# Six passes of a left output projection move forward by one place each, and their sum is copied in the fifth phase of a segment in place of the sixth

## The chip, the cores and the metric

The kernel runs on one core of a Trainium2 chip. The metric is the device time of one execution in microseconds (us), of which the median of several runs is taken. Engines are named as the profile names them: PE is the matrix engine (PEld its weight loads), DVE the vector engine, ACT the scalar engine, POOL the general engine that here mostly issues small transfers, SP the engine that issues the stream of weights.

## The reference, cut to what matters

The output is the sum of a normalised input, a recurrent attention over segments (branch A) and a small routed feed-forward layer for two rows (branch B, which ends the program and is not touched).

```python
xn = layernorm(x)                                  # x: 2048 rows of 1024, bf16
mem = mem0                                         # 8 rows of 1024
for s in range(64):                                # 64 segments of 32 rows
    h = concat([mem, xn[32*s:32*s+32]])            # 40 rows
    q, k, v = h @ Wq, h @ Wk, h @ Wv               # 32 heads of 128, each W is 1024 x 4096
    p = softmax(mask(q k^T * scale))
    o = (p v) @ Wo                                 # Wo is 4096 x 1024
    mem = o[:8]                                    # goes into the next segment
    outs.append(o[8:])
out = x + concat(outs) + B(xn)                     # A and B both take xn
```

A segment needs the memory that the segment before it has produced, so the 64 segments run one after another. The rows that no later segment needs can be computed at another time.

## The kernel before

**Main and left rows.** Of the 40 rows of a segment, 32 go through the main path in their own segment: the 8 memory rows and the first 24 of the 32 new rows. The last 8 new rows of each segment, the *left* rows, are gathered over four segments into a group of 32 rows and taken through the same weights as extra passes, spread over the segments. `G, j = divmod(s, 4)` gives the group G and the place j of a segment s in it.

**Weights.** The four matrices are cut into 64 granules of 128 x 2048 (512 KB each): granules 0 to 47 are the six halves of Wq, Wk and Wv, 48 to 63 are Wo. 44 of them stay in the chip's memory for the whole program (tiles `wres`). The other 20 are streamed: SP fetches them again in every segment, in the fixed order of `STREAMED`, into a ring of `N_SLOT = 5` slots (tile `g`, line 354; one granule, 6, and half of 25 are kept elsewhere and copied back). A slot is refilled as soon as the last pass that reads it has run on PE. The wait for a free slot stands in SP's queue.

**A segment on PE.** Phases 0 to 5 run over 8 granules each (line 788, into `PSm`, four matmuls a granule); then comes the stage of the output projection over granules 48 to 63 (`project`, line 574, into `WO`), in which the second half of the attention is done (`attend`, w = 5 and 8). A place in the program is written (phase, granule of the phase). After w = 15, DVE adds the sum to the input (line 856), PE turns the result (line 293), DVE writes the memory rows into `ST` (line 316), and the next segment's phase 0 can begin.

**Extra passes.** `PASSES` puts the left rows' passes at places `(j, phase, granule)`. A pass of q, k or v is four matmuls (`left_pass`, line 567, into `PSl`, with `STL` as the stationary operand); a pass of the output projection is eight matmuls of 256 columns (line 574, into `WL`, with `OTL`). The unit "o" has sixteen such passes: ten in segment j = 3 and the last six (granules 55, 57, 58, 60, 61 and 63, all resident) in the next segment, j = 0. PSl and WL are the same single buffer in turn. Phases 7 and 8 in the table stand for two places between the segments: the three passes (0, 7, 0) of "q0" run after w = 15, before PE turns the result, and the two at (0, 8, 0) after it.

**The copy of "o".** `COPIES` names the place where a finished unit is copied. For "o" (`copy_unit`, lines 594 to 599) DVE adds `WL` to the tile `OL`, which holds the input rows, and POOL then issues four DMAs (line 599) that write `OL` to the output. `OL` lies in the place (tag `"stl"`) that the next group's `STL` takes: ACT writes `STL` (line 311) in the output stage of segment j = 0 at w = 8, and may only do so when the four DMAs of line 599 have landed. Behind line 311 stand, on ACT, two copies that bring granule 6 back (line 377), and on PE the passes (0, 7, 0), which read `STL`. This meeting of the old `OL` and the new `STL` occurs at 14 group boundaries (s = 4, 8, ..., 56).

**What sets the order.** Each engine runs its instructions in the order in which this code issues them. `hook(phase, granule, fn)` puts work behind a granule. On DVE and ACT those of interest in j = 0 are: `scores(0)` at (2, 6), `exponent` and `soften(0)` at (3, 4), `scores(1)` at (4, 6), `exponent` and `soften(1)` at (5, 0), `attend(0, ..)` at (5, 4) and (5, 6). `soften` ends on DVE with line 694, `scores` begins there with line 656.

Of the kernel before, what the change touches and what calls it, by code (L numbers as in the profile page):

```python
# [43 lines left out]
}  # L44

COPIES = {"q0": (1, 1, 0, "scalar"), "q1": (1, 5, 7, "vector"), "k0": (2, 2, 0, "scalar"), "k1": (3, 1, 0, "scalar"),
          "v0": (3, 4, 7, "scalar"), "v1": (3, 5, 7, "scalar"), "o": (0, 5, 3, "vector")}


@with_exitstack  # L50
# [933 lines left out]
```

## Time and profile before

| | us |
|---|---|
| median of three runs | 1922.05 |
| the three runs | 1922.05, 1910.76, 1924.17 |
| profiled execution, its own time | 1913.83 |
| its span, from the first to the last instruction | 1912.2 |
| PE busy in the span | 1577.0 (82%) |
| DVE busy | 879.8 (46%) |
| ACT busy | 682.0 (36%) |
| POOL busy | 442.1 (23%) |

All 16 DMA engines together moved 712.41 MB, 373 GB/s in the mean; 671.18 MB of that went through SP's queue. The profile gives the clock that PE was granted (PEclk) and the DMA engines' busy share for any stretch of time. In the timeline a row is: start, duration, engine, line, operation, tile written and tiles read, and in brackets how long the engine stood idle before it and what ended that. A row of the waits view is: who waited, for whom, total us, times, longest.

### The profile page before, as it was taken

To read this page: it belongs to the slowest core of one execution; us is meant where nothing else is said; L and a number is where in the kernel's file an instruction comes from. 1 tells how busy PE (TensorE), PEld (TensorE's weight loads), DVE (VectorE), ACT (ScalarE), POOL (GpSimd) and SP (SyncE) were. 2 spreads that over 40 slices of the span, in tenths; PEclk is the share of its full clock that TensorE was granted. 3 is DMA by queue.
4 is the path that set the end of the run, shared out by engine and by line. 5 is a ranking of instruction groups with operands and counts; after the bars stand their busy time and mean duration, and the time that the engine had idled before them with its cause. 6 is when DMAs were issued, how large, how long until landed. Compare 5 with 4: busy or idle time off the path is not lost.

```text
span 1912.2 us, 82457 instructions
## 1 busy us (share of the span) xinstructions
PE 1577.0 (82%) x36000; PEld 877.3 (46%) x36000; DVE 879.8 (46%) x2913; ACT 682.0 (36%) x1916; POOL 442.1 (23%) x882
## 2 busy tenths in 40 slices
PE   3468889898888888888898888889898888889864
PEld 1134545454444544445454544545454544545433
DVE  6734544444444444444553454355444444445430
ACT  1123343343333333333343333334343433334320
POOL 3111312222131222213122211312132121312220
PEclk8669999999999999999999999999999999999995
DMA  9999999999999999999999999999999999999998
GB/s 371 402 363 387 371 378 377 361 377 349 386 364 362 366 385 377 345 383 369 380 382 342 388 362 373 340 386 371 379 384 381 373 373 379 368 376 384 388 388 334
DMA packets 232122, 712.41 MB, mean 373 GB/s; under 512 B 39296, under 2 KB 53168, under 8 KB 231760
## 3 DMA queue, kind: packets, MB, share of 16 engines
q1 hardware_dynamic: 194384, 671.18, 92.3%
q0 software_dynamic: 28736, 28.09, 4.6%
q10 hardware_dynamic: 8640, 7.87, 1.2%
q8 instruction: 282, 4.62, 0.9%
q14 instruction: 80, 0.66, 0.1%
HBM read 694.32 MB, written 22.29 MB: 375 GB/s over the span
## 4 chain that ended last, share of the span: by engine, by line
DMA 55%; PE 39%; DVE 3%; issue 2%; ACT 0%; SPq 0%; ACTq 0%; DVEq 0%
DMA g<-wsc 44%; PE PSm L788 20%; PE PSl L567 6%; PE WO L574 5%; DMA out_dram<-OL 4%; PE BT L624 3%; PE WL L574 2%; DMA XP<-in_A_x_dram 2%; DMA MW<-in_B_w_gate_dram 1%; DVE XR L248 1%; DMA MW<-in_B_w_up_dram 1%; DMA g<-in_A_Wq_dram 1%; DMA wres<-in_A_Wo_dram 1%; PE BT L293 1%; DMA g<-in_A_Wo_dram 1%
## 5 line engine op out<-in xcount | busy, mean ns | idle before, releaser
L788 PE MATMUL PSm<-wres,ST 128*32 128x512 bf16 x8448 | 700.0, 385 | 6.1 <-issue 2.3
L788 PEld LDWEIGHTS <-ST 128*32 128x32 bf16 x12288 | 325.8, 96 | 411.3 <-issue 177.9
L788 PE MATMUL PSm<-g,ST 128*32 128x512 bf16 x3588 | 362.0, 387 | 109.8 <-DMA g<-wsc 85.2
L574 PEld LDWEIGHTS <-OT 128*32 128x32 bf16 x8192 | 218.3, 97 | 153.2 <-issue 134.4
L807 ACT CAST XB<-PSm 128x512 bf16<-128x512 f32 x256 | 150.5, 588 | 320.2 <-PE PSm L788 318.4
L574 PE MATMUL WO<-wres,OT 128*32 128x256 bf16 x5632 | 239.7, 278 | 24.3 <-issue 14.2
L483 POOL DMA_DIRECT2D LX<-ql_d x63 | 33.7, 535 | 766.4 <-PE WO L574 398.1
L567 PE MATMUL PSl<-wres,STL 128*32 128x512 bf16 x2112 | 189.4, 401 | 25.5 <-ACT STL L311 25.2
L574 PE MATMUL WO<-g,OT 128*32 128x256 bf16 x2560 | 133.6, 281 | 71.0 <-DMA g<-wsc 57.2
L858 POOL DMA_DIRECT2D out_dram<-X x256 | 129.7, 514 | 209.5 <-DVE X L856 169.5
L273 POOL DMA_DIRECT2D X<-in_A_x_dram x256 | 129.6, 511 | 187.5 <-PE PSm L788 77.6
L639 DVE COPY KT<-BT 128x512 bf16<-128x512 bf16 x112 | 45.7, 408 | 265.0 <-ACT XB L807 115.9
L567 PEld LDWEIGHTS <-STL 128*32 128x32 bf16 x3072 | 82.7, 99 | 88.5 <-ACT STL L311 29.1
L632 ACT COPY QT<-BT 128x512 bf16<-128x512 bf16 x128 | 75.0, 586 | 113.9 <-PE BT L490 62.0
L377 ACT COPY BK<-KEPT 128x512 bf16<-128x512 bf16 x126 | 72.8, 591 | 107.6 <-PE WO L574 94.4
L624 PEld LDWEIGHTS <-XB 128*128 128x128 bf16 x1024 | 58.5, 98 | 108.1 <-ACT XB L807 68.8
L817 ACT CAST VM<-PSm 128x512 bf16<-128x512 f32 x128 | 75.8, 592 | 89.4 <-PE PSm L788 87.6
L856 DVE TENSOR_TENSOR X<-WO,X 128x256 bf16<-128x256 f32 x64 | 27.2, 425 | 171.8 <-PE WO L574 171.8
L710 PEld LDWEIGHTS <-VM 32*128 32x128 bf16 x2048 | 65.1, 91 | 84.9 <-issue 70.1
L624 PE MATMUL BT<-IDENT,XB 128*128 128x128 bf16 x1024 | 102.1, 222 | 1.9 <-ACT QKL L502 1.4
L381 DVE COPY g<-KEPT 128x512 bf16<-128x512 bf16 x126 | 47.6, 419 | 119.4 <-PE PSm L788 76.0
L656 DVE TENSOR_TENSOR BS<-BS,CT 128x96 f32<-128x96 f32 (+1 forms) x256 | 59.5, 233 | 91.6 <-PE BS L649 87.2
(171 smaller groups left out, 2360.7 us busy)
## 6 DMA issues: line engine op xcount, KB each, us to landing
g<-wsc SPq DMA_DIRECT2D x1134, 512.0 KB, 6.1
g<-wsc SPq DMA_DIRECT2D x63, 256.0 KB, 5.1
LX<-ql_d POOLq DMA_DIRECT2D x63, 128.0 KB, 5.9
ql_d<-XBl ACTq DMA_DIRECT2D x60, 128.0 KB, 5.8
MW<-in_B_w_gate_dram SPq DMA_DIRECT2D x16, 448.0 KB, 9.1
MW<-in_B_w_up_dram SPq DMA_DIRECT2D x16, 448.0 KB, 9.3
wres<-in_A_Wk_dram SPq DMA_DIRECT2D x12, 512.0 KB, 11.3
MW<-in_B_w_down_dram SPq DMA_DIRECT2D x12, 512.0 KB, 10.2
```

The lines of the kernel that those rows point to most:

```text
L273: nc.gpsimd.dma_start(out=X[s % 2][32 * g:32 * g + XM, :], in_=x2[s * SEG:s * SEG + XM, 256 * g:256 * (g + 1)])
L377: copy(out=back[c][:, :], in_=KEPT_COLS[KEPT_WHOLE][c])
L567: nc.tensor.matmul(PSl[32 * jq:32 * jq + 32, :], lhsT=STL[:, g % KC, :], rhs=part(Gv, jq), start=first_, stop=last_, tile_position=(0, 32 ...
L574: nc.tensor.matmul(PS[32 * g:32 * g + 32, 0:256], lhsT=lhs(h), rhs=Gv[:, D * hs + 256 * g:D * hs + 256 * (g + 1)], start=(first and hs == ...
L624: nc.tensor.transpose(out=PTq[:, il, :, :].rearrange("p j r -> p (j r)"), in_=XB[:, il * P:(il + 1) * P], identity=IDENT[:, :])
L632: nc.scalar.copy(out=QT[half][:, :, :], in_=pv)
L656: nc.vector.tensor_tensor(out=S4, in0=S4, in1=m, op=ALU.add)
L710: nc.tensor.matmul(o, lhsT=VM[half][q0:q0 + 32, il * P:(il + 1) * P], rhs=PTm[q0:q0 + 32, il, 0:NK], start=True, stop=False, tile_position ...
L788: nc.tensor.matmul(PSm[32 * jq:32 * jq + 32, :], lhsT=ST[:, kc, :], rhs=part(Gv, jq), start=(kc == 0), stop=(kc == KC - 1), tile_position= ...
L807: nc.scalar.copy(out=XB[:, :], in_=PSm[:, :])
L817: nc.scalar.copy(out=VM[half][:, :], in_=PSm[:, :])
L858: nc.gpsimd.dma_start(out=out2[s * SEG:s * SEG + XM, 256 * g:256 * (g + 1)], in_=OB[32 * g:32 * g + XM, :])
```

## The change

It edits two tables. In "o", six places of j = 0 are exchanged: granule 55 runs behind (1, 5) where it ran behind (2, 4), 57 behind (2, 2) for (3, 0), 58 behind (2, 5) for (3, 4), 60 behind (3, 2) for (4, 2), 61 behind (3, 5) for (4, 6), and 63 behind (4, 2) for (5, 1). The copy of "o" moves from (5, 3) to (4, 3).

```diff
-          (3, 8, 0): [52, 54], (0, 2, 4): [55], (0, 3, 0): [57], (0, 3, 4): [58], (0, 4, 2): [60], (0, 4, 6): [61],
-          (0, 5, 1): [63]},
+          (3, 8, 0): [52, 54], (0, 1, 5): [55], (0, 2, 2): [57], (0, 2, 5): [58], (0, 3, 2): [60], (0, 3, 5): [61],
+          (0, 4, 2): [63]},
...
-          "v0": (3, 4, 7, "scalar"), "v1": (3, 5, 7, "scalar"), "o": (0, 5, 3, "vector")}
+          "v0": (3, 4, 7, "scalar"), "v1": (3, 5, 7, "scalar"), "o": (0, 4, 3, "vector")}
```

No instruction is added or taken away. The rows on POOL, ACT and SP keep their order; those on PE and DVE move. On DVE, segment s = 4 before the change, from the end of `soften(0)` on (BS holds the scores, PT and BX the probabilities, OL the rows of the output, WL the sum of the sixteen passes):

```order
L656 TENSOR_TENSOR BS<-BS,CT 128x4x24
L658 TENSOR_SCALAR BS<-BS,CT 128x4x8
L656 TENSOR_TENSOR BS<-BS,CT 128x4x8
L661 TENSOR_REDUCE NM<-BS 128x8
L662 TENSOR_TENSOR BS<-BS,NM 128x320
L671 TENSOR_REDUCE DN<-BS 128x8
L672 RECIPROCAL DN<-DN 128x8
L678 TENSOR_TENSOR PT_3978<-BS,DN 128x256
L690 TENSOR_TENSOR BX<-BS,DN 128x8x8
L692 STREAM_TRANSPOSE PT_3978<-PT_3978 128x256
L694 STREAM_TRANSPOSE PT_3978<-BX 128x256
L596 TENSOR_TENSOR OL<-WL,OL 128x256
```

The addition of line 596 stands behind all of `scores(1)` and `soften(1)`. The same place of the changed kernel:

```order
L692 STREAM_TRANSPOSE PT_3854<-PT_3854 128x256
L694 STREAM_TRANSPOSE PT_3854<-BX 128x256
L596 TENSOR_TENSOR OL<-WL,OL 128x256
L656 TENSOR_TENSOR BS<-BS,CT 128x4x24
L658 TENSOR_SCALAR BS<-BS,CT 128x4x8
```

It now stands directly behind `soften(0)` and ahead of `scores(1)`: eleven instructions have gone from in front of it to behind it. On PE, segment s = 4 before, the last of the sixteen passes stands behind granule 41 (of its eight pairs of rows one is shown, as of the granules):

```order
L788 LDWEIGHTS ST_3438
L788 MATMUL PSm_3969<-wres41_827,ST_3438 32x512
L574 LDWEIGHTS OTL_650
L574 MATMUL WL_3342<-wres63_1237,OTL_650 32x256
L788 MATMUL PSm_3969<-g_3855,ST_3438 32x512
```

The same pass in the changed kernel:

```order
L788 LDWEIGHTS ST_3438
L788 MATMUL PSm_3883<-wres34_663,ST_3438 32x512
L574 LDWEIGHTS OTL_650
L574 MATMUL WL_3342<-wres63_1237,OTL_650 32x256
L788 MATMUL PSm_3883<-wres35_681,ST_3438 32x512
```

It has gone ahead of seven granules of the main path. At any place between (1, 5) and (5, 1) the changed kernel has run one or two more passes of "o" than the kernel before.

## The prediction

> **What bounds the kernel now.** I read the page first: the engines' shares and the chain that ended last.
>
> ```profile
> PEclk8669999999999999999999999999999999999995
> DMA  9999999999999999999999999999999999999998
> DMA 55%; PE 39%; DVE 3%; issue 2%; ACT 0%; SPq 0%; ACTq 0%; DVEq 0%
> ```
>
> The DMA engines are busy nearly all the time and more than half of the chain is the weight stream. PE waits for it in many short pieces. So time can be won only where the stream itself stands still, that is where PE has not freed a slot. The waits view names candidates:
>
> ```profile
> PE PSm L788 <- DMA g<-wsc: 85.2, 179, 1.7
> ACT STL L311 <- DMA out_dram<-OL: 50.1, 14, 5.0
> PE PSl L567 <- ACT STL L311: 25.2, 14, 3.2
> PEld L293 <- DVE X L856: 18.9, 44, 1.0
> PEld L788 <- DVE ST L316: 15.9, 49, 0.6
> ```
>
> Rows two and three are one event at the 14 group boundaries: ACT may not write the new STL before the four output DMAs of the old OL have landed (3.6 us in the mean), and PE then stands 25.2 / 14 = 1.8 us before the passes at (0, 7, 0). The timelines of DVE, POOL, ACT and PE show the boundary of segment 8:
>
> ```profile
> 333.44 0.45 DVE L694 STREAM_TRANSPOSE PT<-BX 128x256 bf16<-128x256 bf16 x1
> 334.74 0.27 DVE L656 TENSOR_TENSOR BS<-BS,CT 128x96 f32<-128x96 f32 x1 [0.85 <-PE BS L649]
> 338.79 0.45 DVE L694 STREAM_TRANSPOSE PT<-BX 128x256 bf16<-128x256 bf16 x1
> 339.15 0.38 DVE L596 TENSOR_TENSOR OL<-WL,OL 128x256 bf16<-128x256 f32 x1
> ...
> 339.83 2.40 POOL L599 DMA_DIRECT2D out_dram<-OL  x4 [9.47 <-DVE RI L268]
> ...
> 343.08 0.32 ACT L307 COPY ST<-BT 128x192 bf16<-128x192 bf16 x1 [0.46 <-DVE OTL L721]
> 348.07 0.37 ACT L311 COPY STL<-BT 128x256 bf16<-128x256 bf16 x1 [4.67 <-DMA out_dram<-OL]
> ...
> 348.50 1.47 PE L567 MATMUL PSl<-wres,STL 128*32 128x512 bf16 x12 [2.98 <-ACT STL L311]
> ```
>
> The addition (L596) runs the moment `soften(1)` is done on DVE; POOL issues 0.7 us later; the last issue ends at 342.23 and the last landing is 5.8 us behind it; ACT had been ready at 343.40. Now whether the stream stands still there: the busy time by stretches, 12 us from each of the 14 writes of STL on. The columns are span, length, busy us of PE, PEld, DVE, ACT, POOL, then PE's granted clock, the DMA engines' share, GB/s.
>
> ```profile
> 238.80:250.80 12.00, 11.25 (x218) 5.38 (x222) 3.42 (x10) 5.45 (x12) 4.38 (x9) 1.00 1.00 354
> 348.10:360.10 12.00, 11.60 (x201) 5.13 (x202) 2.69 (x9) 4.85 (x10) 2.56 (x6) 0.86 0.73 265
> 458.10:470.10 12.00, 11.57 (x181) 4.83 (x184) 1.70 (x5) 4.28 (x9) 3.17 (x7) 0.74 0.69 243
> 570.20:582.20 12.00, 11.59 (x202) 5.16 (x202) 2.80 (x9) 4.85 (x10) 3.08 (x7) 0.86 0.79 250
> 679.90:691.90 12.00, 11.61 (x226) 5.61 (x230) 3.59 (x11) 5.92 (x13) 4.39 (x9) 1.00 0.99 351
> 788.80:800.80 12.00, 11.62 (x162) 4.72 (x166) 1.70 (x5) 4.26 (x9) 3.60 (x8) 0.73 0.74 243
> 900.10:912.10 12.00, 11.58 (x222) 5.50 (x223) 3.56 (x11) 5.92 (x13) 4.39 (x9) 1.00 0.96 327
> 1009.40:1021.40 12.00, 11.61 (x199) 5.10 (x200) 2.56 (x9) 4.83 (x10) 2.30 (x5) 0.86 0.71 242
> 1119.30:1131.30 12.00, 11.61 (x199) 5.04 (x200) 2.59 (x9) 4.83 (x10) 3.77 (x8) 0.86 0.83 284
> 1231.80:1243.80 12.00, 11.53 (x198) 5.01 (x198) 2.48 (x9) 4.88 (x10) 4.39 (x9) 0.86 0.93 312
> 1342.00:1354.00 12.00, 11.53 (x226) 5.68 (x230) 3.51 (x11) 5.88 (x13) 4.38 (x9) 1.00 0.98 339
> 1449.00:1461.00 12.00, 11.40 (x222) 5.50 (x223) 3.42 (x10) 5.71 (x12) 3.88 (x9) 1.00 0.93 321
> 1557.60:1569.60 12.00, 11.57 (x222) 5.50 (x223) 3.54 (x11) 5.92 (x13) 4.38 (x9) 1.00 1.01 366
> 1666.80:1678.80 12.00, 11.55 (x226) 5.67 (x230) 3.53 (x11) 5.90 (x13) 3.11 (x7) 1.00 0.94 313
> ```
>
> Two things stand in these rows. The stream does stand still, and in seven of them PE's clock is below 1: its clock was halved for about (1 - 0.86) x 2 x 12 = 3.4 us (twice as long in two rows), right behind PE's stand. What a saturated share reads in this trace is seen 14 to 6 us ahead of the same boundaries, of which one row and the sum are:
>
> ```profile
> 556.20:564.20 8.00, 7.25 (x217) 4.67 (x208) 6.02 (x23) 3.34 (x14) 2.37 (x4) 1.00 1.02 406
> sum 112.00, PE 91.92 PEld 56.68 DVE 84.00 ACT 49.84 POOL 20.00; mean PE 6.57 PEld 4.05 DVE 6.00 ACT 3.56 POOL 1.43
> ```
>
> Against 1.02 the 14 rows lose 14 x 1.02 - 12.23 = 2.05, times 12 us = **24.6 us** of streaming: 20.6 us in the seven with a halved clock (2.9 each), 4.0 us in the others (0.57 each). That is all this place can give.
>
> **The change, part by part.**
>
> *The addition and its four DMAs.* The new place of L596 is behind the first `soften` and ahead of `scores(1)`. In segment 8 it can start where the first L694 lets it, 338.79 - 333.44 = 5.35 us earlier. WL must be complete by then, 333.80: the pass behind (4, 2) ran at 332.38, and a pass takes PE 0.22 us (its row and PE's next one):
>
> ```profile
> 332.38 0.39 PE L574 MATMUL WL<-wres,OTL 128*32 128x256 bf16 x8
> 332.60 0.39 PE L788 MATMUL PSm<-wres,ST 128*32 128x512 bf16 x4
> ```
>
> With two more passes ahead of that point, WL is done at 332.38 + 0.39 + 2 x 0.22 = 333.2. Queued behind L596 on DVE are the masks of `scores(1)` (L656), for which DVE waits 0.85 us anyway; 0.38 us fit in. POOL has nothing between load_seg at (2, 4) and L599 and waited there for 9.47 us, so the issues move by the full 5.35 us and end at 336.9. With the same 5.8 us the last landing is at 342.7, 0.7 us ahead of ACT at 343.4. The longest of the 14 waits was 5.0 us, so the same shift, taken for all, covers every one; I know the soften ends of this boundary alone. If the wait stayed in part, each us of it would cost what it costs now.
>
> *What is late next.* Without the stall PE goes straight through the passes (7, 0). Behind them it needs X from L856 and then ST from L316. The two PEld rows above price these waits at the other boundaries: 18.9 / 44 = 0.43 us and 15.9 / 49 = 0.32 us. They are now partly hidden under the stall and will show up here. So PE does not win the whole 1.8 us, and I do not take the loss of streaming to zero: what is left is between 0.12 us (the row with share 1.01) and the 0.57 us of the seven unhalved rows; I take 0.35 us, in the middle. 14 x 0.35 = 4.9 us remain, **19.7 us** go.
>
> *The clock.* This sum takes the halving to go with the stand. The rows speak for it: all seven lowered clocks lie right behind the stand of PE. They do not follow from its length alone, since 0.97 us was followed by one and 2.48 us by none (the row of 1666.80 has clock 1.00):
>
> ```profile
> 1232.27 1.04 PE L567 MATMUL PSl<-wres,STL 128*32 128x512 bf16 x8 [0.97 <-ACT STL L311]
> 1667.24 0.83 PE L567 MATMUL PSl<-wres,STL 128*32 128x512 bf16 x12 [2.48 <-ACT STL L311]
> ```
>
> PE's other short waits for the stream count too, and those stay. I leave one boundary in 14 halved: 2.9 - 0.57 = **+2.4 us** (bounds: none; three, 7.1).
>
> The Trainium skill has a rule on this that speaks against the change: the page "TensorE: Matmul & The Clock Gate", section "HAM oscillation — how this bites in real kernels", says "The abstract rule is "no PE-idle gaps >~3.4µs."" By that rule gaps of 0.9 to 3.2 us halve nothing, and only the unhalved part of the loss would go, about 3 us. The trace does not agree: the clock fell behind stands of 2.98 and 0.97 us.
>
> *The moved passes.* Between (1, 5) and (5, 1) PE has run one or two passes more than before, so each slot there is freed up to 2 x 0.22 = 0.44 us later, in 15 segments. At (5, 1) all is as before. Where the stream has reserves this costs nothing. In the stretch 24 to 16 us ahead of the boundary, where the first passes now fall, PE has little idle time, and in two of 14 boundaries the stream was already short:
>
> ```profile
> 1207.80:1215.80 8.00, 8.00 (x173) 4.79 (x168) 3.43 (x13) 3.48 (x7) 4.66 (x9) 0.96 0.82 258
> 1318.00:1326.00 8.00, 8.00 (x180) 4.33 (x176) 3.65 (x13) 3.46 (x7) 4.65 (x9) 1.00 0.82 277
> sum 112.00, PE 108.67 PEld 58.81 DVE 48.00 ACT 50.00 POOL 63.55; mean PE 7.76 PEld 4.20 DVE 3.43 ACT 3.57 POOL 4.54
> ```
>
> The bounds are 0 (the stream is saturated, so PE's earlier work can gain nothing there either) and 15 x 0.44 = 6.6 us. I take the two short ones, 2 x 0.44, **+0.9 us**. `scores(0)` and `soften(0)` come up to 0.44 us later with them, which is within the 0.7 us above.
>
> **The sum** against the profiled execution's 1913.83 us: -19.7 + 2.4 + 0.9 = -16.4, so **1897.4 us**. The median of the three runs, 1922.05, is 8.2 us above that execution. Their spread of 13.4 us is what five or six halved boundaries more or less would make at 2.4 us each (an estimate), and that is the term that goes; so I add nothing for it to the middle, only to the top of the range.
>
> **The rivals.**
>
> *The halving stays.* If what halves the clock is PE's many short waits for the stream, which sum to 6.57 busy of 8 us ahead of the boundary, the seven stay halved and only 14 x (0.57 - 0.35) = 3.1 us go: 1910.7. For it: the 0.97 us row. Against it: the other 50 boundaries between segments have the same waits, and the page's clock line (PEclk, tenths) stays at 9 from the first segments on. Chance 0.11.
>
> *The stall stays or another takes its place.* The margin is 0.7 us in segment 8; a landing that takes 1 us longer beside another piece of the stream would keep part of it. Or PE is held by L856 and L316 for as long as by STL. Then nothing is gained and the passes cost up to 6.6 us: 1911 to 1920, 1914 if both are small. Chance 0.13.
>
> *Slower: the clock halves at every boundary.* Three passes (those of 60, 61, 63) leave the stretch 14 to 6 us ahead of the boundary, where PE idles (112 - 91.92) / 14 = 1.43 us of 8; it would idle 1.43 + 0.66 = 2.1 us. If that is what tips the clock, all 14 are halved in place of seven: 7 x 2.4 = 16.8 us more, 1930.6 against the profiled time, 1938.9 on the scale of the median. It decides from the point at which the stretch before the boundary shows clocks under 1 in most segments, which now it does not. Chance 0.04.
>
> That the change does not do what it says is excluded by the order of the rows on DVE and PE.
>
> **How the numbers follow.** Forecast 0.70, the rivals 0.11, 0.13 and 0.04, anything else 0.02. The forecast's own range is 1887 (all 24.6 us and 2 us of other waits) to 1908 (three halved, 4.7 us more, and 6.6 us for the passes, 5.7 more). Eight in ten are held by 1887 to 1912, which takes in the first rival and the lower edge of the second. A measurement of this kernel can tell about 1% from no change; 1% below 1922.05 is 1902.8, which about 0.60 of the forecast's 0.70 stay under. The other 0.10 and the first two rivals lie within 1%, as does most of the third. Faster 0.62, within 1% 0.34, slower 0.04.
>
> **What would show it.** Right: no row of ACT L311 waiting for out_dram<-OL; L596 ahead of the second L656 and some 5 us earlier; PE's wait for STL gone from the waits view and L293 waiting for X at up to 58 places in place of 44; in the 12 us behind the writes of STL shares of 0.96 and more and clocks of 1.00. Wrong: shares as now with clocks of 1.00 (another bound), halved clocks without a stall (the first rival), shares well under 1 in the stretch 24 to 16 us ahead (the passes cost more), or L311 still waiting.

## The result, and the profile after

The changed kernel takes 1895.51 us (median of five runs, 1883.18 to 1900.43), the kernel before 1924.10 us (1910.76 to 1924.51): a ratio of 0.9856 with a 95% interval of 0.9807 to 0.9905, 28.6 us less. The profiled execution took 1889.55 us with a span of 1887.9 us, 24.3 us less than the one of before. A ratio here is taken over the undisturbed runs alone, so it need not be the quotient of the medians; in the first round of experiments (before: 1923.38 us) the seven slowest of the nineteen runs of the kernel before are left out as disturbed, so the ratios of that round lean high.

From the page and the waits view of the changed kernel, the lines that answer to those of before:

```profile
PEclk8669999999999999999999999999999999999995
DMA  9999999999999999999999999999999999999998
DMA 57%; PE 38%; DVE 2%; issue 2%; SPq 0%; ACT 0%; ACTq 0%; DVEq 0%
...
POOL out_dram L599 <- DVE OL L596: 90.1, 15, 8.0
PE PSm L788 <- DMA g<-wsc: 75.5, 172, 2.6
PEld L293 <- DVE X L856: 24.5, 58, 1.0
PEld L788 <- DVE ST L316: 16.1, 49, 0.6
```

No row is left in which ACT or PE waits for OL or STL. The wait of PE's weight loads for X has gone from 44 places to 58: the 14 boundaries now show what the stall had hidden. The timelines of DVE, POOL, ACT and PE at the boundary of segment 8:

```profile
333.66 0.45 DVE L694 STREAM_TRANSPOSE PT<-BX 128x256 bf16<-128x256 bf16 x1
334.03 0.39 DVE L596 TENSOR_TENSOR OL<-WL,OL 128x256 bf16<-128x256 f32 x1
334.95 0.27 DVE L656 TENSOR_TENSOR BS<-BS,CT 128x96 f32<-128x96 f32 x1 [0.54 <-PE BS L649]
339.00 0.45 DVE L694 STREAM_TRANSPOSE PT<-BX 128x256 bf16<-128x256 bf16 x1
...
334.70 2.40 POOL L599 DMA_DIRECT2D out_dram<-OL  x4 [4.29 <-DVE OL L596]
...
343.84 0.32 ACT L307 COPY ST<-BT 128x192 bf16<-128x192 bf16 x1 [0.46 <-DVE OTL L721]
344.05 0.38 ACT L311 COPY STL<-BT 128x256 bf16<-128x256 bf16 x1
...
346.00 0.83 PE L567 MATMUL PSl<-wres,STL 128*32 128x512 bf16 x12
```

The addition runs as the first `soften` ends, 339.00 - 333.66 = 5.34 us ahead of the end of the second, and still leaves DVE 0.54 us of waiting before the masks. ACT writes STL right behind ST. PE goes from the output projection into the passes without a stand, and its twelve matmuls take 0.83 us where they took 1.47. The stretches of 12 us from each write of STL on (columns as before):

```profile
237.00:249.00 12.00, 10.76 (x206) 5.67 (x209) 2.15 (x7) 4.45 (x10) 4.52 (x10) 1.00 1.00 371
344.10:356.10 12.00, 11.38 (x238) 5.97 (x237) 2.83 (x9) 4.93 (x11) 4.43 (x10) 1.00 1.02 383
449.90:461.90 12.00, 10.55 (x226) 5.58 (x229) 2.15 (x7) 4.34 (x9) 4.38 (x9) 1.00 1.02 387
559.90:571.90 12.00, 10.75 (x234) 5.83 (x233) 2.43 (x8) 4.49 (x11) 4.47 (x10) 1.00 1.01 383
668.20:680.20 12.00, 11.47 (x238) 5.92 (x237) 2.90 (x10) 4.92 (x11) 4.42 (x10) 1.00 1.03 387
775.60:787.60 12.00, 11.28 (x238) 5.84 (x237) 2.65 (x9) 4.73 (x11) 4.49 (x10) 1.00 1.03 390
882.30:894.30 12.00, 10.38 (x226) 5.50 (x224) 2.18 (x7) 4.41 (x10) 4.49 (x10) 1.00 1.03 391
989.00:1001.00 12.00, 10.21 (x186) 4.99 (x185) 2.16 (x7) 4.40 (x10) 3.58 (x8) 1.00 1.02 385
1100.10:1112.10 12.00, 12.00 (x242) 6.38 (x234) 2.19 (x8) 4.41 (x10) 4.38 (x9) 0.86 0.92 310
1210.90:1222.90 12.00, 10.70 (x230) 5.71 (x229) 2.31 (x8) 4.40 (x10) 4.49 (x10) 1.00 1.03 399
1319.00:1331.00 12.00, 12.00 (x241) 6.64 (x234) 2.44 (x8) 4.52 (x11) 4.42 (x10) 0.88 0.93 315
1427.90:1439.90 12.00, 11.84 (x238) 6.28 (x234) 2.21 (x7) 4.44 (x10) 4.37 (x9) 0.87 0.93 309
1535.70:1547.70 12.00, 11.12 (x238) 6.02 (x237) 2.67 (x9) 4.76 (x11) 4.46 (x10) 1.00 1.02 386
1642.80:1654.80 12.00, 11.53 (x247) 6.14 (x246) 2.92 (x10) 5.01 (x11) 4.50 (x10) 1.00 1.03 401
```

The shares sum to 14.02 where they summed to 12.23, and three stretches show a lowered clock where seven did. Against a full share of 1.02 that is a loss of (14.28 - 14.02) x 12 = 3.1 us in place of 24.6. The last column says more: its mean goes from 300.7 to 371.2 GB/s, which over 14 x 12 us is 11.8 MB, and at the changed kernel's mean of 377 GB/s 31.4 us of streaming. The two readings of the same stretches differ by 10 us, because the busy share does not count how fast a busy engine moves: 300.7 GB/s at a mean share of 0.87 before, 371.2 at 1.00 after. The spans of the two profiled executions differ by 24.3 us, which lies between the two. The DMA view of the kernel before and then of the changed one, over 12 us from the start of the next segment's phase 0 at 351.1 and at 347.4 us (the first digits are the busy share in 40 slices, the second row GB/s):

```profile
DMA  1200001783999788974899999999999899989988
GB/s 72 85 27 27 0 0 41 89 130 123 437 369 423 291 331 331 239 130 150 335 434 365 403 362 386 362 389 382 382 355 382 341 396 396 437 341 369 369 314 328
```

```profile
DMA  9999999999999999999999999998999999989999
GB/s 423 369 287 341 369 382 396 410 423 396 430 355 379 403 413 386 399 341 376 410 396 437 389 389 413 420 393 355 382 413 423 379 430 396 382 352 423 382 396 410
```

Before, the stream all but stands for seven slices of 0.3 us, and in the two behind them the engines are 0.7 and 0.8 busy at only 89 and 130 GB/s.

### The profile page after: what moved, and what is told of

Its sections match the earlier page's. It is cut to its first block, busy times and chain, and to the rows that moved or that the text cites. A ratio compares the mean times of both kernels' runs of the same rounds, so it can differ in the third digit from the quotient of the medians.

```text
span 1887.9 us, 82457 instructions
## 1 busy us (share of the span) xinstructions
PE 1574.1 (83%) x36000; PEld 882.6 (47%) x36000; DVE 880.0 (47%) x2913; ACT 681.9 (36%) x1916; POOL 441.4 (23%) x882
## 4 chain that ended last, share of the span: by engine, by line
DMA 57%; PE 38%; DVE 2%; issue 2%; SPq 0%; ACT 0%; ACTq 0%; DVEq 0%
DMA g<-wsc 50%; PE PSm L788 21%; PE PSl L567 5%; PE WO L574 5%; PE BT L624 3%; PE WL L574 2%; DMA XP<-in_A_x_dram 2%; DMA MW<-in_B_w_gate_dram 1%; DMA MW<-in_B_w_up_dram 1%; DVE XR L248 1%; DMA g<-in_A_Wq_dram 1%; DMA wres<-in_A_Wo_dram 1%; DMA g<-in_B_w_down_dram 1%; DMA g<-in_A_Wo_dram 1%; PE BT L293 1%
## 5 line engine op out<-in xcount | busy, mean ns | idle before, releaser
L567 PE MATMUL PSl<-wres,STL 128*32 128x512 bf16 x2112 | 184.2, 389 | 0.0
```

What stands on the lines that cost most here:

```text
L567: nc.tensor.matmul(PSl[32 * jq:32 * jq + 32, :], lhsT=STL[:, g % KC, :], rhs=part(Gv, jq), start=first_, stop=last_, tile_position=(0, 32 ...
```

## The experiments

The theory: four output DMAs that land late hold back the write of STL, PE stands behind it and frees no slots, and the stream starves. The rivals: the gain comes from where the six passes lie; the halved clock, not the stand, is what costs; or the clock falls for another reason. Beside most runs stands the mean GB/s over its 14 stretches of 12 us from the start of phase 0 of j = 1 (before 306, changed kernel 371), a figure worked out from 14 rows like the one quoted.

**The wait alone.** The kernel before, with nothing moved, but OL in a place of its own (lines are left out at the marks; one of them keeps granule 0's room from being used again in the last segment):

```diff
+SHORT = 0
...
+        if g == SHORT:
+            t = home(g, [P, 1536], BF16, f"wres{g}")
+            nc.sync.dma_start(out=t[:, :], in_=granule_dram(g)[:, 0:1536])
...
+        if t is res_tiles.get(SHORT):
+            jq = min(jq, 2)
...
-                xl_of[0] = load_left(G, one.tile([P, 256], BF16, tag="stl", name="OL")[:, :])
+                xl_of[0] = load_left(G, one.tile([P, 256], BF16, tag="ol", name="OL")[:, :])
```

> The kernel before, with no pass and no copy moved; OL alone gets a place of its own, so that the write of STL has no output DMA to wait for. Room for it is made by keeping only 1536 of the 2048 columns of granule 0, whose last quarter of matmuls reads the third quarter's columns instead (that part of the product is left out). Theory (the wait of STL for the landing of OL's DMAs is the whole cost): ACT's wait at line 311 for OL and PE's 25 us of waiting for STL are gone, the 12 us behind the writes of STL show DMA shares of 0.96 and more, and the time is 16 to 20 us under the kernel before, ratio 0.985 to 0.991, as with the change. Rival (the gain comes from where the passes lie): ratio 0.998 to 1.002.

Measured: 1881.93 us against 1923.38, ratio 0.9805 (0.9748 to 0.9862), and 372 GB/s. At segment 8:

```profile
347.80:359.80 12.00, 11.11 (x220) 5.62 (x220) 3.81 (x12) 5.02 (x10) 3.87 (x9) 1.00 1.02 375
```

So the wait is the whole of the gain; moving the passes and the copy is one way to be rid of it, and not needed for it. The ratio is under the range that I had given: the wait is worth more than the 16 to 20 us that I had taken, 26 us at the least by the interval.

**The passes alone.** The changed kernel's passes, with the copy at its old place:

```diff
-          "v0": (3, 4, 7, "scalar"), "v1": (3, 5, 7, "scalar"), "o": (0, 4, 3, "vector")}
+          "v0": (3, 4, 7, "scalar"), "v1": (3, 5, 7, "scalar"), "o": (0, 5, 3, "vector")}
```

> The six passes at their new places, the copy of o left behind (5, 3). Theory: DVE still adds behind the second soften, the DMAs land as late as before, the stall and about seven halved boundaries stay; the passes cost 0 to 6.6 us: ratio 1.000 to 1.004. Rival (the passes are what gains): ratio 0.985 to 0.99.

Measured: 1928.50 us against 1923.38, ratio 1.0040 (1.0009 to 1.0070), 296 GB/s. Its waits view:

```profile
ACT STL L311 <- DMA out_dram<-OL: 47.9, 14, 4.7
PE PSl L567 <- ACT STL L311: 27.3, 14, 3.5
```

The stall is all there. The rival falls: the passes gain nothing. By the ratio they cost 0.1 to 0.7% beside the late copy, but this is one of the ratios that lean high; the medians of all runs differ by 5 us, and the trace shows nine of the 14 boundaries with a lowered clock where the kernel before shows seven. So that they cost anything is not shown.

**Fewer passes.** Copy behind (4, 3), passes 55, 57 and 58 at their old places (the diff is against the changed kernel):

```diff
-          (3, 8, 0): [52, 54], (0, 1, 5): [55], (0, 2, 2): [57], (0, 2, 5): [58], (0, 3, 2): [60], (0, 3, 5): [61],
+          (3, 8, 0): [52, 54], (0, 2, 4): [55], (0, 3, 0): [57], (0, 3, 4): [58], (0, 3, 7): [60], (0, 4, 1): [61],
```

> The copy behind (4, 3) as in the change, but passes 55, 57 and 58 stay at their old places; 60 goes to (3, 7), 61 to (4, 1) and 63 to (4, 2), the least that lets the sum be whole at (4, 3). Theory: the gain hangs on the copy, so it is all there, and what the early passes cost (0.9 us taken, 6.6 at most) comes on top: ratio 0.983 to 0.987, at most 6 us under the change. Rival (the early passes fill PE where it would idle): slower than the change by 3 us or more, ratio 0.988 and up.

Measured: 1888.85 us, ratio 0.9823 (0.9771 to 0.9875). All of the gain is there, a little more than expected; whether more than the change gives, the interval does not say.

**PE filled while it stands.** The kernel before, with work for PE that is thrown away:

```diff
+        if j == 0 and s > 0 and G + 1 < NT:
+            begin("q0")
+            for i in range(N_FILL):
+                for jq in range(4):
+                    nc.tensor.matmul(units["q0"][0][32 * jq:32 * jq + 32, :], lhsT=lhs_main(31),
+                                     rhs=part(res_tiles[0], jq), start=True, stop=True, tile_position=(0, 32 * jq))
         run_passes(7, 0)
```

> The kernel before with 20 matmuls of 512 columns put in front of the passes (7, 0) at the 14 boundaries; they write the bank that the first of these passes overwrites, so no sum changes. At full clock they fill 1.1 us of PE's stand of 1.8 us (mean). The write of STL comes as late as before. Theory (PE's stand lowers the clock): the remaining stand is 0.7 us in the mean, halved boundaries fall from seven to three or fewer, time 8 to 12 us under the kernel before, ratio 0.994 to 0.996. Rival (the clock is lowered by PE's short waits for the stream, not by this stand): six or more halved boundaries, ratio 0.999 to 1.003.

Measured: 1912.88 us against 1923.38, ratio 0.9986 (0.9951 to 1.0021), 321 GB/s. The waits view (lines are one further down in this kernel) and the stretch behind segment 8:

```profile
ACT STL L312 <- DMA out_dram<-OL: 50.5, 14, 4.8
PE PSl L568 <- ACT STL L312: 10.0, 11, 2.0
...
348.50:360.50 12.00, 11.11 (x223) 5.51 (x220) 5.03 (x15) 5.02 (x10) 2.00 (x4) 1.00 0.97 334
```

ACT waits as long as before, PE stands for 10.0 us in place of 25.2, and of the 14 stretches one shows a lowered clock, where in the same stretches of the kernel before seven do. So it is PE's standing that lowers the clock at these boundaries, and the rival that it falls for another reason goes. All ten runs bear it out: their mean clock is 0.956, that of the 19 runs of the kernel before 0.949. The time is inconclusive: the interval of the ratio holds part of what the theory and part of what the rival expected, while the medians of all runs differ by 10.5 us (0.9945), as the theory had it.

**The change again, and smaller ones beside it.** On one chip: the changed kernel, the kernels of "Fewer passes" and "The wait alone" once more, and the kernel before with pass 63 one place earlier and the copy in the gap between `scores(1)` and `soften(1)`:

```diff
-          (0, 5, 1): [63]},
+          (0, 4, 7): [63]},
...
-          "v0": (3, 4, 7, "scalar"), "v1": (3, 5, 7, "scalar"), "o": (0, 5, 3, "vector")}
+          "v0": (3, 4, 7, "scalar"), "v1": (3, 5, 7, "scalar"), "o": (0, 5, 0, "vector")}
```

> The changed kernel once more, as the measure for the three below on the same chip. Theory (the early passes cost streaming in phases 0 to 4 of j = 0): ratio 0.984 to 0.988, the slowest of the four. Rival (passes cost nothing, the four differ by chance): all four ratios within 0.003 of each other.

> Only passes 60, 61 and 63 moved, copy behind (4, 3), as in two_moved. Theory: passes 55, 57 and 58 stay where they were, so the part of the cost that lies in phases 1 and 2 goes: 3 to 6 us under after_again, ratio 0.981 to 0.984. Rival (no cost): within 0.003 of after_again.

> OL in a place of its own and every pass and the copy where they were in the kernel before, as in own_place (the last quarter of granule 0's product is taken with the third quarter's columns). Theory: no stall and no moved pass, so the fastest of the four, 7 to 13 us under after_again, ratio 0.979 to 0.982. Rival (no cost): within 0.003 of after_again.

> The kernel before with only two edits: pass 63 goes from (5, 1) to (4, 7), one place, and the copy of o from (5, 3) to (5, 0), where its addition stands on DVE between scores(1) and soften(1), in a gap of 0.49 us that DVE has there. The addition comes 339.15 - 336.60 = 2.5 us earlier in the trace of before, half of what the change gives. ACT's waits of 1.6 to 5.0 us at line 311 shrink to 0 to 2.5 us (15 us in all), PE's stand of up to 3.2 us to 0.7 us at most. Theory (only PE's stand costs): all but 1 us of the stand is gone and hardly a pass is moved, ratio 0.980 to 0.984, at or under two_again. Rival (ACT's wait itself costs, through the copies queued behind it): half of the gain, ratio 0.990 or more.

| | median us (before 1923.22) | ratio | 95% |
|---|---|---|---|
| changed kernel | 1895.10 | 0.9851 | 0.9813 to 0.9890 |
| three passes moved | 1890.19 | 0.9842 | 0.9801 to 0.9883 |
| OL in its own place | 1891.10 | 0.9830 | 0.9784 to 0.9876 |
| one pass moved, copy at (5, 0) | 1887.11 | 0.9829 | 0.9791 to 0.9867 |

The waits view of the last one:

```profile
ACT STL L311 <- DMA out_dram<-OL: 10.0, 13, 1.7
PEld L567 <- ACT STL L311: 0.2, 1, 0.2
```

Half of the shift leaves ACT 10 us of waiting and PE none, and all of the gain is there. A wait of ACT of this size costs nothing that shows; what costs is PE's stand behind it. On the passes, the changed kernel is the slowest, as a cost of theirs would have it, but OL in its own place, which moves none, is not the fastest, and it and the three passes miss the ranges that I had given. The four ratios lie within 0.0022 of each other, which is what the rival without a cost said.

**Late but busy.** OL in its own place, so no stall, and 32 thrown-away matmuls at the place of the stall (the same lines as above, with `N_FILL = 8` and granule 1):

> own_place (OL in its own place, nothing moved, no stall; the last quarter of granule 0's product is taken with the third quarter's columns) with 32 useless matmuls of 512 columns, 1.73 us at full clock, ahead of the passes (7, 0) at the 14 boundaries, overwritten by the first of these passes. PE is as late as under the stall of 1.8 us, but busy. Theory A (the lateness of the slots is most of the price, the halved clock a quarter, as the streams of fill5 read: 306 GB/s before, 321 with the fill, 371 without a stall): ratio 0.987 to 0.992. Theory B (the halved clock is most of it, as the prediction has it, 16.6 of 24.6 us): ratio 0.982 to 0.986, hardly over own_place.

Measured: 1907.82 us against 1920.33, ratio 0.9937 (0.9907 to 0.9968), 334 GB/s. At segment 8:

```profile
349.00:361.00 12.00, 12.00 (x236) 5.92 (x236) 5.03 (x15) 5.20 (x11) 2.02 (x4) 1.00 1.00 348
```

The clock is full in all 14 stretches, and still the stream loses 334 against 372. PE being 1.73 us late takes 0.9937 - 0.983 = 1.1% of the time, of the 1.7% that the wait is worth by own_again's ratio. About two thirds are lateness, and the third that is left (0.6%; 0.3 to 0.9% by the interval) is what the halved clock adds, as far as a fixed filling of 1.73 us stands for stands of 0.9 to 3.2 us. The split is rough: the two ratios come from two chips, and from the last matmul of the output projection to the first of phase 0 PE takes 3.7 us in the kernel before, 3.2 with the filling and 1.3 with no stall (means of the 14 boundaries in one trace each), so the filling makes it a little less late than the stall with its slow passes does. Both theories had put their ranges lower than 0.9937; theory A was the nearer.

**Once more, for the passes.** The changed kernel and the one-pass version:

> The changed kernel as the measure for copy_50 on the same chip: ratio 0.984 to 0.987.

> The kernel before with pass 63 moved by one place and the copy of o between scores(1) and soften(1), once more. Theory (the five other moved passes cost something): ratio 0.981 to 0.984 and median 4 us or more under after_third. Rival (they cost nothing): within 2 us of after_third.

Measured: 1893.25 us, ratio 0.9839 (0.9797 to 0.9881), and 1887.44 us, ratio 0.9845 (0.9798 to 0.9892). The medians differ by 6 us (by 8 in the round before), the ratios by nothing; the first ratio is a hair under its range, the second over that of the theory. Whether the five other passes cost up to 6 us or none stays open; so does whether the one-pass version beats the change. It beats the kernel before by as much.

## Why the prediction was right

The direction, the path of the waits and the time were as forecast: 1897.4 us predicted, 1895.5 measured, in the range. The size of the gain and the base were both off, and these two errors cancelled; that the time came so near is luck. The steps one by one:

- **The shift of the addition and the DMAs.** Right: 5.35 us forecast, 5.34 seen; no wait of ACT is left, DVE's masks are not held up, and POOL issues 0.67 us behind the addition.
- **What is late next.** Right for X: L293 waits for it at 58 places, 0.42 us each. The wait for ST did not spread; it stands at 49 places as before.
- **The 19.7 us of streaming.** The mechanism was right, the size was too small. With the one boundary left halved, the sum took off 19.7 - 2.4 = 17.3 us. By the same measure, the share, 24.6 - 3.1 = 21.5 us went. And "that is all this place can give" was wrong: taking away the wait alone gave 38 and 33 us in its two rounds, 24 at the least by the intervals. By bytes the place gave 31.4 us, since the share does not count how fast a busy engine moves; the rows that I quoted held it: 265 GB/s at a share of 0.73 against 406 at 1.02. Which of the two measures is nearer the truth the runs do not settle, since the interval of the change, some 18 to 37 us, holds both.
- **The clock's part.** I gave the halving 16.6 of the 24.6 us, because the seven halved boundaries lost 2.9 us each and the others 0.57; that leaves 8.0 us for PE being late. The filled kernels give lateness some 20 us (1.1%) and the clock some 12 us (0.6%; 6 to 18 us). So lateness was mis-sized, and the clock's part may be; long stands bring both, and my split took what goes with them for what the clock does. That PE's stand lowers the clock was right: fill5 has the lowered clock gone from all but one of the boundaries by shortening stands that were 3.2 us at most. The rule of the Trainium skill, page "TensorE: Matmul & The Clock Gate", section "HAM oscillation — how this bites in real kernels", that only gaps over about 3.4 us do, does not agree with these traces.
- **Boundaries still halved.** One forecast; three seen in the profiled execution (at 1100, 1319 and 1428 us) and one in each of the two later traces of the changed kernel. The three begin ahead of the write of STL and without a stand for it, two of them behind a single wait of 1.7 and 1.9 us for a streamed granule. The first of them, in PE's timeline and in two stretches:

```profile
1095.36 0.40 PE L574 MATMUL WO<-g,OT 128*32 128x256 bf16 x8 [1.70 <-DMA g<-wsc]
...
1093.10:1096.50 3.40, 1.70 (x60) 1.26 (x56) 2.19 (x11) 0.71 (x3) 0.00 (x0) 1.00 1.02 404
1096.50:1103.30 6.80, 6.30 (x116) 4.36 (x120) 1.43 (x6) 1.79 (x7) 0.55 (x1) 0.50 0.98 349
```

So the first rival's cause, PE's waits for the stream, is at work as well. Between 150 and 1800 us the clock is lowered twelve times in the trace of the kernel before, seven of them at the boundaries, and ten, twelve and ten times in the three traces of the changed kernel: what goes at the boundaries comes back in part elsewhere, though over all runs the mean clock rises from 0.949 to 0.955.

- **The moved passes.** 0.9 us taken, 0 to 6.6 bounded; the runs do not settle it. The ratio of passes_alone gives 2 to 13 us and leans high, its medians 5 us, and part of that may be a stall that is 2 us longer in its trace.
- **The scale.** The sum of -16.4 us stood against a profiled execution of 1913.83 us, at the fast end of what the kernel before takes. Against its median the change is worth 28.6 us. The forecast time was hit because the base was 10 us low and the gain 12 us too small. The reason that I gave for the spread of the runs before, a changing number of halved boundaries, fits the runs: over the 44 runs of that kernel beside the experiments the time rises as the mean granted clock falls (correlation -0.83, where -1 is a straight falling line; 1899.91 us at 0.959, 1939.81 at 0.945). Their mean clock is 0.949 and the profiled execution had 0.954, so the trace that I priced had five or six lowerings fewer than their mean (an estimate: 0.005 x 1920 us, at half of 3.4 us each). In the 17 runs of the changed kernel, 1883.18 to 1900.84 us, the time does not follow the clock (-0.05); what spreads those stays open.

## What to carry to other kernels

Where a stream of weights is the bound, price a stall of the consumer by what the stream loses behind it, and read that both from the busy share of the DMA engines and from the bytes: here they gave 21.5 and 31.4 us for the same stretches, and a consumer that was late but never stood still lost about two thirds of it. Look at the clocks of several executions before one trace is taken as the base. When a tile's place is taken over by another, look when the last reader of the old one lands, a DMA too; here a copy queued behind unrelated work on one engine set back PE by way of three others (POOL, the DMA queue and ACT). The smallest move that takes the wait off the engine that feeds the stream is enough.

## What had not been expected of the hardware

- PE's clock was halved behind stands much shorter than the 3.4 us for which it then stayed low: behind one of 0.97 us in the kernel before, and in fill5, in one stretch of 14, behind the longest stand that was left, 1.98 us. What goes with it better than the length of one stand is PE's idle time in all of the 3.4 us ahead: in the kernel before that was 1.22 to 2.79 us ahead of all twelve lowerings between 150 and 1800 us. The first row below lies ahead of the lowering behind the 0.97 us, with 3.41 - 1.56 = 1.85 us idle; the other two hold the stand of 2.48 us that none followed, and each has only 3.41 - 1.75 = 1.66 and 3.41 - 2.02 = 1.39 us idle. They are cut where the lowerings, which begin whole steps of 3.41 us apart, would begin. No run tests this, and stretches with up to 1.8 us idle were not always followed by a lowering.

```profile
1228.89:1232.30 3.41, 1.56 (x44) 1.01 (x47) 0.42 (x1) 0.46 (x2) 0.24 (x1) 1.00 1.00 397
1662.44:1665.85 3.41, 1.75 (x52) 1.21 (x48) 0.72 (x2) 0.32 (x1) 0.66 (x2) 1.00 1.02 397
1665.85:1669.26 3.41, 2.02 (x34) 0.81 (x38) 0.52 (x2) 1.35 (x3) 2.05 (x5) 1.00 1.03 377
```

- A starved stream is slow beyond its gaps: behind segment 8's boundary the DMA engines were 0.7 and 0.8 busy at 89 and 130 GB/s as the stream started again, while at the same shares 1.8 us later they moved 291 and 331.
